# A new order table for a gated linear attention and gMLP kernel on one core

## The chip, the cores and the metric

The kernel runs on one core of a Trainium2 chip. The metric is the device time of one execution in microseconds (us); the median over runs is compared. A core has a matmul engine (TensorE, "PE" in the profile, with its weight loads as "PEld"), a vector engine (VectorE, "DVE"), a scalar engine (ScalarE, "ACT"), GpSimd ("POOL") and SyncE ("SP"), which only issues DMAs here. Each engine works through its own queue in order and waits for the others by semaphores. Matmuls write to PSUM, eight banks that DVE and ACT read; everything else lies in SBUF.

## The reference

Gated linear attention (a recurrence over time with a decay per key channel), and then a gMLP block with a spatial gating unit, on float32 inputs:

```python
B, H, S, D = 4, 8, 768, 48                      # attention
state = zeros(B, H, D, D)
for t in range(S):
    state = alpha[:, :, t, :, None] * state + einsum('bhd,bhe->bhde', k[:, :, t], v[:, :, t])
    y[:, :, t] = einsum('bhd,bhde->bhe', q[:, :, t], state)
x = y.transpose(0, 2, 1, 3).reshape(B, S, H * D)    # 4 x 768 x 384
h = maximum(x @ w_in, 0)                            # w_in 384 x 1024
u, v = h[..., :512], h[..., 512:]
v_n = (v - mean(v)) / sqrt(var(v) + 1e-6)           # over the last axis
v_s = einsum('ts,bsd->btd', w_spatial, v_n) + b_spatial[None, :, None]   # 768 x 768
out = (u * v_s) @ w_out                             # 512 x 384
```

## The kernel before

**Tiling.** A sequence of 768 is cut into six chunks of 128 steps; the four batches give 24 chunks, numbered 0 to 23 (chunk i belongs to batch i // 6). Inside a chunk the recurrence is done as matmuls: sums of log(alpha) along time, their exponentials folded into q and k, a masked score matrix, and a state that is carried from chunk to chunk. Chunks 0 to 9 are handled as pairs 0 to 4 (pair j is chunks 2j and 2j+1, their steps interleaved by parity), chunks 10 to 23 as singles. The names of the operations:

- Loads on SP: `ac`, `kc`, `qc`, `vc` are alpha, k, q and v of a pair, 384 KB each (with an `s` at the end: of a single, 192 KB). Three buffers of each kind, by pair number. `w_in.1`, `w_in.0`, `w_sp.0` to `w_sp.2`, `w_out` are weights of 768 KB, through two raw buffers, so that each waits for the `cast` operations of the one two before. `b_sp` is a small load that POOL issues.
- `ln` (ACT) takes the logarithm of alpha, `cum` (PE) sums it along time into a bank (with `tot`, the total, for pairs 3 and 4, whose second parity `c1` adds on DVE), `einv` and `eexp` (ACT) make exp(-sum) and exp(sum), the second in place in the bank, `ebc` (ACT) makes the exponential of the total from the same bank. A pair has each of `cum`, `einv`, `eexp` twice, by parity; so pair 0 has `einv.0.0` and `einv.0.1`.
- `kt` (POOL or DVE) and `qt` (DVE, out of the bank) multiply k and q; `vb` casts v. `tr.q`, `tr.k` (for a single `trk`) transpose on PE, `ev` (single: `evs`) copies out of PSUM on DVE or ACT.
- `sc` (PE) makes scores, `m` (single: `ms`, DVE) masks them, four per pair and two per single; `upd` (PE) makes the update of the state, `z` (DVE) adds the old state, `S` (POOL or DVE) scales it, `sb` casts it. `ya` (PE) is the part of a pair inside its chunks, `y` (PE) the part from the old state (for a single all of it), `xe` (ACT or DVE) copies the result out as the block's x.
- `v` and `u` (PE) are the two halves of the first projection, `ve` and `ue` (ACT or DVE) their relu, `bn` (DVE), `rs` (ACT) and `vn` (DVE) the normalisation. `s` (PE) mixes along time, in two parts; `se` (DVE) adds the bias, `g` (POOL or DVE) multiplies with u, `o` (PE) is the last projection, `oe` the copy out of its bank, `st` the store on SP. `s.b.d.h.m` has batch, feature tile, half of the time axis, part; `o.b.t` has batch and time tile.
- Set-up: `zeros` (DVE), `ident`, `tri`, `causal`, `one` (POOL) make masks and padding; `wt` (PE) transposes the spatial weights, `we` (ACT or DVE) copies them out; `bb` and `be` spread the spatial bias. `causal` must be over before the first `m` of a pair, `bb` needs the load `b_sp`.

**Order.** The whole program is 955 operations. A list of them is built in the order of the algorithm, each with the engines that may do it, the operations that it depends on and the PSUM banks that it takes. The order in which they are issued is a table written by a search outside the kernel: a string of words such as `P108@0:512#0`, that is engine letter (P PE, D DVE, A ACT, G POOL, S SP), number in the list, after `@` the bank or banks that it takes, and after each `:` a filler matmul of so many float32 columns into the bank named behind `#`. Filler keeps PE busy early on and computes nothing. The function that walks the table takes each word, asserts that dependencies and banks are met, and emits the instructions; each engine's queue then has its operations in the order of the table. The scheduler of the framework is switched off by `ctx.enter_context(tc.manual_schedule())`; it still sets a semaphore wait wherever two engines touch the same data, and where two engines read one PSUM bank.

The table before starts with pair 1, then pair 0, then pair 2; its first two lines:

```python
D2 D0 G4 S103 A107 P108@0:512#0:472#0 A110 S105 A111 D116 G5 G8 S53 S104 D1 G6 G7 P109@1 A112 A113 D3 D119
P124@0,2:512#2:384#2 D115 A57 P59@3 A62 A64 A114 D118 D126 P121@4,5 P58@6 A60 A63 A61 D122 D125 S54 D123 D68
```

Of the kernel before, what the change touches and what calls it, by code (L numbers as in the profile page):

```python
# [38 lines left out]


PLAN = """
D2 D0 G4 S103 A107 P108@0:512#0:472#0 A110 S105 A111 D116 G5 G8 S53 S104 D1 G6 G7 P109@1 A112 A113 D3 D119
P124@0,2:512#2:384#2 D115 A57 P59@3 A62 A64 A114 D118 D126 P121@4,5 P58@6 A60 A63 A61 D122 D125 S54 D123 D68
P134@5,0:384#7 S55 S162 S56 D69 P137@1,4 G65 D66 P74@6,3:400#7 A75 D136 D135 P49@2 P71@0,7 A72 D76 D73 P84@7,0:296#6
D139 D50 S9 S164 A166 P167@3 G67 G70 P77@2,4 P168@5 S106 S163 A10 A173 A169 A170 S13 D86 P87@0,6 D85 D89 D88
P90@0,6:512#7:112#7 A91 A171 G11 D78 G79 D12 P94@0:416#7 D138 D80 D175 S165 A172 G117 P92 A93 D81 D120 G82 G174 D178
P127@4,3 P183@6,1 P97@5 A185 A184 D177 P140@1,2 G83 P141 P180@6,7 D128 D129 G130 P51@4 G14 D95 D131 D182 A181 D96 P143
G179 D16 A144 A15 P193@6,7 D194 A142 P156@2 P190@3,0 A98 A52 D191 D195 D192 A157 P148@1 P150@5 G176 G132 A149 A133
D158 P186@3 P145@2 A146 P196@0,1 P154@7 D187 D188 S17 S20 G18 D147 P197 P152@3 D153 P31@2,4 D33 D99 G189 G21 G22 P199
A151 A19 A198 D155 P201@0 A200 A32 A159 A202 A100 D161 P214@1 A215 P204@2 P37@4,3 A38 P34@0,7 P216@5 P212@1 A36 D160  # L50
A217 S23 S319 A205 P40@4,6 A41 D101 D35 D39 D102 P230@7 P226@2 P218@4 D203 A42 G25 G24 P46@6,5 P222@3 D206 A207 D209
D208 S268 A213 D47 P43@1,0 P223 D224 D48 P227 A323 P231 D232 P219 P324@3 S26 G225 G233 D45 A272 A44 D228 P274@5 P273@1
P325@0 D275 P238@7 P239 P242@2 D326 S269 A331 A28 D220 G229 D27 G29 G221 D240 G241 S270 S321 P243 P246@4 P247 A276
A327 A278 A277 A30 A279 A280 D284 D244 P210@7 D248 D282 G281 P234@2 P235 D236 A328 S320 S271 G249 P253@1 A211 A329
A330 D333 D285 P287@7,4 G245 G237 A289 D288 D335 D336 P250@2 P290@5,3 D292 S379 P256@7 P341@4,6 S322 D343 A291 A251
A257 A254 P300@3,2 S403 G332 A342 G286 P303@0,5 P338@6,7 D301 D302 D305 P259@1 G283 P293@3,4 D294 G295 G296 A339 A340
G334 G337 S380 S381 P354@7,2 P351@5,6 S404 S405 S382 S570 S489 S406 A260 A383 P262@1 A263 P384@3 D304 S490 S572 D352
D297 D356 D355 P265@0 A385 S513 S491 S492 S546 S571 P306@1,5 P308 A407 A387 A309 A386 P344@2,4 P408@7 P313@5 D307
P310@1 G298 G299 G388 D353 D345 A409 G346 G347 S516 S515 S514 S611 G411 D266 D389 A314 D315 A311 A410 D412 D312
P357@2,6 P358 P391@1,3 P360 A359 S547 S548 S635 A393 A392 S613 S549 S612 P367@2 P365@3 A361 P398@1,7 A316 P414@0,5  # L60
D348 P373@6 G390 D400 D399 D318 P394@4 P369@7 A415 A416 A574 A374 A370 P417@1,5 S573 P371@0 S637 S636 P362@6 A372 A493
A363 P575@7 G349 G350 D395 P401@0 A402 G396 G413 D418 D419 D397 P420@5 P494@6 P422@0 D375 D364 A421 A576 D368 D317
P425@5 P431@2 A376 A423 D378 D377 A426 A497 D424 A495 A366 A577 P437@1 D427 A428 A432 A500 D438 D429 D430 A517 P451@0
A578 A496 A550 P443@5 P447@3 P439@4 P433@2 A434 G498 G579 P444 P448 P440 D580 D445 P435@7 P463@5 P464 P452 P518@2 A436
D441 D446 D449 A519 A520 D499 G442 P501@3,7 P582@6,4 D453 G454 D450 A583 A502 A521 A615 A524 P459@0 P504@1 D503 D505
D465 D523 P460 P467@6 P468 P551@5 D469 P508@1,3 G522 D461 P525@2,7 A552 A527 A526 D584 D509 D510 S614 S721 S638 A554
P471@6 P455@0 P456 P528@1 D457 A553 A472 P474@2 G466 G506 G462 A475 G555 P616@0 A639 A617 P532@6,3 D556 D529 P558@5,4
P589@2,7 S722 S745 D533 G458 G470 G507 G557 G620 P477@1 D590 D534 D591 S748 S724 S747 S723 S746 S778 P486@6 A560 A618
A478 A559 A619 A487 D621 P483@2 P561@1 A484 D530 G531 P511@7 D562 P535@5 P565@6,0 P623@3,4 D566 D567 D625 D624 A512
P640@2 G563 P537@7 A536 A641 P480@6 A538 A642 G581 S802 S781 S779 A564 P540@0 P585@3 G643 S780 D644 D586 S843 S804  # L70
S803 P568@4 P592@2 P630@3,7 P646@5,1 A541 A569 D542 P599@4 A593 S844 A648 A647 G622 P605@2 D539 P626@1 A606 A725 A481
A543 G587 G588 D631 P649@5,0 P594@3 P597@2 D627 D651 D632 G628 G629 G645 S845 S867 S805 P601@6 S868 S869 P726@7 P633@0
D650 A600 A595 P652@3 A727 A634 A749 D607 A653 P603@5 D596 D545 D544 A608 P654@0 A655 P657@3 D610 D609 A598 A658 D656
P665@4 A666 A728 A604 P750@0 P671@2 D659 A660 D661 D662 P667@3 D731 D732 A751 A753 A668 G756 A752 G730 G754 D755
P683@4 P663@5 A664 A602 A782 P679@1 P672 P669@3 D670 P684 D685 P680 P736@6 P675@3 P699@4 A729 D737 G738 D686 D681 G682
P783@6 P757@7,0 P733@1,5 P676 A784 A758 A786 A785 A734 A806 A759 A735 D673 D739 D674 D677 P760@2 P700 P695@7 P696 G789
G787 P691@3 P692 D761 G678 D701 D788 D697 G702 D693 P807@0 P790@6,4 D792 P740@5,7 P764@1,2 D765 D742 A808 A809 P687@3
P703@4 A847 A791 P793@6 P848@7 P688 P706@1 A704 A851 G698 P709@4 D812 A849 A810 A707 A850 G694 G762 D766 D794 D689
G811 G852 G763 P814@3,0 G795 G690 G813 D741 P797@1,6 P767@5 A710 A816 P743@4 A768 G796 D853 D815 P855@7,2 P821@3,0
D798 A744 A871 P772@5 D823 D799 D822 P769@4 P872@0 P817@6 A773 A857 A770 D818 D856 D774 P712@5 P715@3 P800@7 A873 A874  # L80
G875 A801 P824@6 D876 P862@4,2 P878@0,1 A825 A880 P833@7 D771 D879 P837@6 P829@0 D864 D863 S485 S846 S488 S870 S476
A713 G819 A775 A834 A830 A838 G820 G854 P858@2 D859 G860 G861 S255 S261 S708 S267 S252 S479 S714 S711 P881@5,1 S705
P718@4 P826@6 D882 D883 A877 A827 P865@5 P884@1 P835@6 D839 D828 A866 P886@5 P831@2 A885 A840 P889@1 P895@0 D887 D776
A832 P899@2 A836 A890 D777 D841 D842 A716 P915@1 P911@3 P919@6 P907@5 D888 D891 A892 D719 D894 D896 D893 P897@4 P903@7
P904 P916 P908 D905 G906 D898 P920 D917 P923@7 D909 D921 D922 S720 S482 S264 S473 S258 G910 S717 G918 P901@4 P912 D913
A902 A900 P927@5 P928 P931@2 D914 P924 P934@3 P940@4 A941 S942 P932 A935 S936 P937@6 A938 S939 D925 G926 D929 D930
D933 P949@4 A950 P952@2 P943@3 D944 A953 S954 S951 S945 P946@2 A947 S948
"""


# [867 lines left out]
```

## Time and profile before

| | |
|---|---|
| median of 3 runs (lowest to highest) | 145.87 us (145.28 to 146.18) |
| the profiled execution: its time, its span | 145.72 us, 143.9 us |
| granted PE clock over the span | 0.997 |
| busy time PE, PEld, DVE | 134.8, 80.6, 124.2 us |
| busy time ACT, POOL | 104.4, 81.1 us |
| matmuls, of them filler | 2225, 20 |
| moved by DMA | 28.66 MB |

The span runs from the first to the last instruction that the profiler saw; the execution's own time is 1.8 us longer. A busy time is the union of an engine's instructions, and matmuls overlap in the pipeline, so what an operation costs PE is better read as the distance from its start to the next one's start. A line of a group or a wait names engine, tile and line of the program, and most copies share one helper's line; the tile tells which operation it is (`vs` is written by `se`, `ptm` by `m` and `ms`, `kqT` by `ev`, `bc` by `ebc`, `binv` by `einv`, `zs` by `z`, `state` by `S`, `bank` by PE).

### The profile page before, as it was taken

To read this page: it belongs to the slowest core of one execution; us is meant where nothing else is said; L and a number is where in the kernel's file an instruction comes from. 1 tells how busy PE (TensorE), PEld (TensorE's weight loads), DVE (VectorE), ACT (ScalarE), POOL (GpSimd) and SP (SyncE) were. 2 spreads that over 40 slices of the span, in tenths; PEclk is the share of its full clock that TensorE was granted. 3 is DMA by queue.
4 is the path that set the end of the run, shared out by engine and by line. 5 is a ranking of instruction groups with operands and counts; after the bars stand their busy time and mean duration, and the time that the engine had idled before them with its cause. 6 is when DMAs were issued, how large, how long until landed. Compare 5 with 4: busy or idle time off the path is not lost.

```text
span 143.9 us, 5488 instructions
## 1 busy us (share of the span) xinstructions
PE 134.8 (94%) x2225; PEld 80.6 (56%) x2225; DVE 124.2 (86%) x282; ACT 104.4 (73%) x263; POOL 81.1 (56%) x121
## 2 busy tenths in 40 slices
PE   5999998999997999999999999999999999999990
PEld 2455545455564566556657675666656665566550
DVE  3099899999777899999999999998999999898950
ACT  3566384978939896799969998999597989640251
POOL 6063259743469949942538978562399965102610
PEclk9999999999999999999999999999999999999998
DMA  4999999857999999897979999998999964009054
GB/s 112 268 261 266 331 198 321 245 203 268 295 297 239 246 181 180 163 181 133 211 129 206 191 163 201 172 205 140 204 190 196 308 225 148 28 0 328 0 179 152
DMA packets 84841, 28.66 MB, mean 199 GB/s; under 512 B 79568, under 2 KB 83280, under 8 KB 84816
## 3 DMA queue, kind: packets, MB, share of 16 engines
q1 hardware_dynamic: 84784, 28.32, 88.0%
q8 instruction: 17, 0.28, 0.9%
q14 instruction: 8, 0.07, 0.1%
q0 software_dynamic: 32, 0.00, 0.0%
HBM read 23.60 MB, written 4.72 MB: 197 GB/s over the span
## 4 chain that ended last, share of the span: by engine, by line
PE 51%; ACT 8%; DVE 7%; issue 2%; DVEq 0%
PE bank L720 36%; PE bank L690 3%; DVE vs L855 3%; PE bank L662 2%; PE bank L706 2%; PE bank L372 2%; ACT v_sb L182 1%; PE bank L629 1%; DVE gT L187 1%; ACT uT L182 1%; PE bank L678 1%; PE bank L484 1%; PE bank L550 1%; ACT xT L176 1%; PE bank L527 1%
## 5 line engine op out<-in xcount | busy, mean ns | idle before, releaser
L720 PE MATMUL bank<-w_spT,vn 128*128 128x384 bf16 x192 | 35.6, 327 | 1.2 <-DVE vs L855 1.2
L187 POOL TENSOR_TENSOR gT<-vs,uT 128x384 bf16<-128x384 f32 x24 | 22.4, 948 | 16.8 <-DVE vs L855 16.7
L720 PEld LDWEIGHTS <-vn 128*128 128x128 bf16 x192 | 17.8, 97 | 12.9 <-issue 1.8
L187 POOL TENSOR_TENSOR kt<-kc,binv 128x384 bf16<-128x384 f32 x18 | 18.2, 1014 | 10.4 <-ACT binv L639 9.7
L187 POOL TENSOR_TENSOR state<-zs,bc 128x384 f32<-128x384 f32 x17 | 14.6, 857 | 10.1 <-DVE zs L350 5.5
L176 ACT COPY kqT<-bank 128x512 bf16<-128x512 bf16 x30 | 16.8, 590 | 4.4 <-PE bank L484 4.0
L720 PE MATMUL bank<-xT,w_in 128*128 128x384 bf16 x96 | 20.0, 327 | 0.0
L720 PE MATMUL bank<-w_in,xT 128*128 128x512 bf16 x72 | 18.9, 381 | 0.6 <-ACT bank L641 0.5
L720 PE MATMUL bank<-w_out_sb,gT 128*128 128x384 bf16 (+1 forms) x100 | 18.5, 321 | 0.2 <-DVE ptm L695 0.2
L695 DVE TENSOR_TENSOR ptm<-bank,mask 128x512 bf16<-128x512 f32 x28 | 17.9, 682 | 0.3 <-PE bank L690 0.2
L855 DVE TENSOR_TENSOR vs<-bank,bsp_bc 128x384 f32<-128x384 f32 x31 | 16.3, 548 | 2.0 <-PE bank L720 2.0
L187 DVE TENSOR_TENSOR qt<-qc,bank 128x384 bf16<-128x384 f32 x24 | 12.9, 546 | 5.3 <-ACT bank L447 4.7
L782 DVE BATCH_NORM_STATS2 stats<-v_sb 128x6 f32<-128x512 bf16 x24 | 16.3, 679 | 0.0
L182 ACT ACTIVATE uT<-bank 128x384 bf16<-128x384 f32 x25 | 11.7, 488 | 4.5 <-PE bank L720 4.4
L182 ACT ACTIVATE v_sb<-bank 128x512 bf16<-128x512 f32 x22 | 13.0, 598 | 2.5 <-PE bank L720 2.4
L535 DVE TENSOR_TENSOR ptm<-bank,mask 128x512 bf16<-128x512 f32 x20 | 12.9, 682 | 0.5 <-PE bank L527 0.4
L720 PEld LDWEIGHTS <-gT 128*128 128x128 bf16 x100 | 8.8, 98 | 5.9 <-issue 0.5
L720 PEld LDWEIGHTS <-w_in 128*128 128x128 bf16 x96 | 8.5, 98 | 6.4
L176 ACT CAST xT<-bank 128x384 bf16<-128x384 f32 x23 | 10.5, 484 | 2.1 <-PE bank L372 2.0
L234 PE MATMUL bank<-junk 128*128 128x512 f32 (+6 forms) x20 | 10.2, 624 | 1.9 <-DVE junk L277 1.8
L178 POOL CAST vb<-vc 128x384 bf16<-128x384 f32 x19 | 9.7, 523 | 3.9 <-DMA vc<-in_v_dram 3.9
L799 DVE TENSOR_SCALAR vn<-v_sb,mvs,rstd 128x512 bf16<-128x512 bf16 x24 | 9.2, 423 | 1.6 <-ACT rstd L793 1.5
(115 smaller groups left out, 246.4 us busy)
## 6 DMA issues: line engine op xcount, KB each, us to landing
ac<-in_alpha_dram SPq DMA_DIRECT2D x14, 192.0 KB, 5.1
kc<-in_k_dram SPq DMA_DIRECT2D x14, 192.0 KB, 4.6
qc<-in_q_dram SPq DMA_DIRECT2D x14, 192.0 KB, 4.3
vc<-in_v_dram SPq DMA_DIRECT2D x14, 192.0 KB, 4.7
raw_w<-in_moe_w_spatial_dram SPq DMA_DIRECT2D x3, 768.0 KB, 4.4
out_dram<-raw_w SPq DMA_DIRECT2D x11, 192.0 KB, 2.2
ac<-in_alpha_dram SPq DMA_DIRECT2D x5, 384.0 KB, 5.6
qc<-in_q_dram SPq DMA_DIRECT2D x5, 384.0 KB, 8.1
```

Source lines behind the costliest of these rows:

```text
L176: nc.scalar.copy(out=out, in_=in_)
L178: ENG[eng].tensor_copy(out=out, in_=in_)
L182: nc.scalar.activation(out=out, in_=in_, func=AF.Relu)
L187: ENG[eng].tensor_tensor(out=out, in0=in0, in1=in1, op=ALU.mult)
L234: nc.tensor.matmul(out=banks[n][:, 0:cols].rearrange("p (a b) -> p a b", a=4), lhsT=junk, rhs=junk[:, None, 0:cols // 4].to_broadcast([128 ...
L535: nc.vector.tensor_tensor(out=ptm[n2][:, par, s], in0=banks[sl.bank].rearrange("p (hp t) -> p hp t", hp=HP), in1=mask[:, par][:, None, :]. ...
L690: nc.tensor.matmul(out=pt[s][:, hp, :], lhsT=kT[rows, hp, :], rhs=qT[rows, hp, :], start=True, stop=True)
L695: nc.vector.tensor_tensor(out=ptm[n2][:, ci, s], in0=banks[sl_p[s].bank].rearrange("p (hp t) -> p hp t", hp=HP), in1=mask[:, 2][:, None, : ...
L720: nc.tensor.matmul(out=ps, lhsT=lhsT, rhs=rhs, start=first and n == 0, stop=last and n == len(pairs) - 1)
L782: nc.vector.bn_stats(out=stats[tt % 2], in_=v_sb[n2][:, tt, :])
L799: nc.vector.tensor_scalar(out=vn[n2][:, x, :], in0=v_sb[n2][:, x, :], scalar1=mvs[n2][:, x, 0:1], scalar2=rstd[n2][:, x:x + 1], op0=ALU.su ...
L855: nc.vector.tensor_tensor(out=vs[d], in0=banks[sl.bank][:, 0:TH], in1=bsp_bc[:, th, :], op=ALU.add)
```

## The change

Only the table is new: the same 955 operations, with other engines, banks and places. The functions that build and emit the operations are the same. The table after was found by a search whose model lets engines that read one PSUM bank wait for each other, and which judged an order with two sets of durations. Its first lines, which hold most of what the prediction walks through:

```diff
-D2 D0 G4 S103 A107 P108@0:512#0:472#0 A110 S105 A111 D116 G5 G8 S53 S104 D1 G6 G7 P109@1 A112 A113 D3 D119
-P124@0,2:512#2:384#2 D115 A57 P59@3 A62 A64 A114 D118 D126 P121@4,5 P58@6 A60 A63 A61 D122 D125 S54 D123 D68
...
+D0 D3 D1 D2 G5 G8 S53 S55 S103 S54 G4 A57 P58@0:512#0:512#0:160#0 A60 P51@1 A52 P59@2 A62 A61 A107 A63 S56 D66 D69
+P74@0,1:512#3:512#3:296#3 P108@3 S104 D65 G70 G6 D68 P71@4,5 A64 A76 A75 P109@1 A112 A110 S162 S105 D67 D72 D73
...
```

In names, the first operations of the new order by engine:

```
SP   ac.0 qc.0 ac.1 kc.0 vc.0 kc.1 ac.2 qc.1 vc.1 w_in.1 kc.2 qc.2 w_in.0 vc.2 ac.3 w_sp.0 qc.3 kc.3 w_sp.1 vc.3 w_sp.2
PE   cum.0.0 bb.1 cum.0.1 tr.q.0 cum.1.0 tr.k.0 cum.1.1 sc.0.1 upd.0 sc.0.0 cum.2.1 tr.k.1 bb.0 ya.0 cum.2.0 tr.q.1 y.1
     upd.1 sc.1.0 sc.1.1 v.0.0 v.0.1 tr.k.2 ya.1 y.3 tr.q.2 y.2 v.0.3 sc.2.1 v.0.2 sc.2.0 u.0.3.0 u.0.2.0 upd.2 u.0.0.0 ya.2
DVE  zeros.0 zeros.3 zeros.1 zeros.2 qt.0.0 qt.0.1 kt.0.0 kt.0.1 vb.0.0 ev.k.0.0 ev.k.0.1 m.0.1.0 m.0.0.1 z.0 S.0 m.0.1.1 z.1 m.0.0.0
ACT  ln.0 einv.0.0 be.1 einv.0.1 eexp.0.0 ln.1 eexp.0.1 ebc.0 ev.q.0.1 ev.q.0.0 einv.1.1 einv.1.0 ln.2 eexp.1.0 ev.k.1.0 ev.k.1.1 eexp.1.1
POOL ident b_sp tri vb.0.1 causal kt.1.1 kt.1.0 sb.0 S.1 cast.w_in.1.0 S.2 kt.2.0
```

and of the old one, on SP and PE:

```
SP   ac.1 qc.1 ac.0 kc.1 kc.0 qc.0 ac.2 vc.0 w_in.1 qc.2 vc.1 kc.2 w_in.0 vc.2 w_sp.0 w_sp.1 w_sp.2 ac.4 ac.3 w_out kc.3
PE   cum.1.0 cum.1.1 tr.q.1 cum.0.1 tr.k.1 cum.0.0 sc.1.0 sc.1.1 tr.q.0 bb.0 tr.k.0 sc.0.0 cum.2.0 upd.0 cum.2.1 sc.0.1 ya.0
     v.0.0 y.1 upd.1 tr.q.2 v.0.1 ya.1 y.2 tr.k.2 bb.1 y.3 sc.2.1 v.0.3 sc.2.0 u.0.0.0 u.0.1.0 upd.2 v.0.2 ya.2
```

Further on, the operations of pair 3 (tr.q.3, tr.k.3, sc.3.1, sc.3.0, upd.3, ya.3) go between batch 0's u, wt and first s, where they were behind all of batch 0's s. At the end PE's order was s.3.3.1.0, s.3.1.1.1, o.3.0, o.3.2, s.3.3.1.1, o.3.1, o.3.5 in two halves, o.3.3, o.3.4; it is now s.3.2.1.1, s.3.3.1.0, s.3.3.1.1, o.3.2, o.3.1, o.3.0, o.3.5.0, o.3.4, o.3.5.1, o.3.3.

Operations by engine, where the count differs (before, after):

| operation | DVE | ACT | POOL |
|---|---|---|---|
| xe | 1, 6 | 23, 18 | |
| ev | 10, 12 | 10, 8 | |
| kt | 6, 3 | | 4, 7 |
| kts | 0, 1 | | 14, 13 |
| cast | 3, 0 | 5, 6 | 8, 10 |
| sb | 3, 1 | 2, 5 | 15, 14 |
| S | 3, 2 | | 17, 18 |
| g | 8, 9 | | 24, 23 |
| vb | 1, 2 | 0, 3 | 9, 5 |
| vbs | 1, 2 | 3, 2 | 10, 10 |
| ue | 7, 6 | 25, 26 | |
| we | 6, 7 | 6, 5 | |
| be | 1, 0 | 1, 2 | |

Filler falls from 4000 columns in ten matmuls to 3656 in ten, the last of it ahead of tr.k.2 (before: of v.0.0).

## The prediction

> **What bounds the kernel now.** I read the busy times first, then the stretches, the chain that ended last, the waits, and last the timeline of each engine, to lay every operation of the table beside its time.
>
> ```profile
> span 143.9 us, 5488 instructions
> PE 134.8 (94%) x2225; PEld 80.6 (56%) x2225; DVE 124.2 (86%) x282; ACT 104.4 (73%) x263; POOL 81.1 (56%) x121
> ...
> PE bank L720 36%; PE bank L690 3%; DVE vs L855 3%; PE bank L662 2%; PE bank L706 2%; PE bank L372 2%; ACT v_sb L182 1%; PE bank L629 1%; DVE gT L187 1%; ACT uT L182 1%; PE bank L678 1%; PE bank L484 1%; PE bank L550 1%; ACT xT L176 1%; PE bank L527 1%
> ```
>
> The chain is mostly PE. But a pipelined PE looks fuller than it is, so I took from the timeline the distance from the start of one PE operation to the next (medians): v 0.653 us, u 0.489, a finished s 0.650 + 0.325, o 0.656, ya 0.668, tr 0.340, trk 0.331, sc about 0.33, a single's y 0.451. Over the 268 operations they add up to 121.7 us; ahead of the last one, 121.0. It starts at 139.40, so PE is then 18.4 us "late": lateness is start time less PE work ahead. It is the number that a new order can change. It is 5.3 at the first cum, 13.4 at the first v, 15.4 from 36 to 45 us, 17.65 at 68 us, and 18.4 at the end. Four fifths are the ramp.
>
> ```profile
> 0.00:5.00 5.00, 3.21 (x4) 1.33 (x5) 1.41 (x16) 1.83 (x2) 2.35 (x12) 1.00 0.66 159
> 5.00:10.00 5.00, 4.82 (x51) 2.39 (x49) 2.75 (x10) 2.90 (x7) 1.59 (x5) 1.00 1.27 261
> 10.00:15.00 5.00, 4.66 (x85) 2.58 (x85) 4.93 (x13) 3.52 (x11) 2.05 (x5) 1.00 1.23 277
> ...
> 60.00:70.00 10.00, 10.00 (x178) 6.05 (x175) 9.54 (x24) 9.82 (x26) 3.97 (x7) 1.00 0.92 174
> ```
>
> Stretches: after the first busy figure (PE) come PEld, DVE, ACT, POOL. DVE is full from 10 us on. Its own start-to-start times (m 0.60 us, qt and z 0.465, bn 0.82, vn 0.32) add up to 120.7 us: as much as PE. So I also count the "lead": DVE work that must be over before a PE operation, less PE work ahead of it. DVE's idle time plus the largest lead is a floor under PE's lateness. Before, the largest lead is 8.1 us, at batch 0's first s (behind vn.0.1), and DVE had idled 7.0 us by 28 us, its start included: 15.1, against a lateness of 15.4 there.
>
> ```profile
> DVE vs L855 <- PE bank L720: 2.0, 4, 0.8
> DVE kt L187 <- ACT binv L444: 0.9, 1, 0.9
> DVE qt L187 <- ACT bc L646: 0.5, 2, 0.3
> PE bank L720 <- ACT bank L641: 0.5, 1, 0.5
> PE bank L720 <- DVE vs L855: 1.2, 2, 0.9
> ```
>
> These waits, with what the chain shows around them, are PE's stalls after the ramp: 1.10 us before s.0.0.1.0 (45.2; a chain se, c1.3, ebc, einv, kt.3.1, se on DVE and ACT), 0.61 at cums.11 (57.0), 0.33 at v.2.0 (86.4), 0.40 at s.2.2.1.1 (105.9): 2.4 us in all.
>
> **The change, part by part.** No instruction is added or taken away, but for the filler: 4000 columns become 3656. Engines: DVE gains five xe (0.465), two ev (0.33) and a few others and loses three kt, three casts, two sb; by rows DVE +0.4, ACT +0.2, POOL +1.8 us. None is worth anything by itself.
>
> Bank reads. Two engines read one bank only where ebc (ACT) and qt (DVE) share it. ebc stands first in 13 of 16 cases in both tables. The row prices this: qt waited for bc twice, 0.5 us. Between 0 and 0.5 us of DVE time can come of it; I take 0. The Trainium skill (PSUM — Partial Sum Buffer, "PSUM bank collisions raise a hardware error") says that two engines on one bank and quadrant must be kept apart, reads against reads too; by that rule, with which the 0.5 us agrees, no order escapes and 0.5 us stays the most; without it the part is worth 0.
>
> Ramp, walked with the rows. zeros.0 now goes first on DVE, so filler starts at about 1.05 instead of 1.79, but ac.0 lands at 4.42 as ac.1 did: the first cum stays at 5.35. The granted clock rose at 6.44, 4.65 us after the first matmul; it may rise by 5.7. (By the Trainium skill, TensorE: Matmul & The Clock Gate, "What's actually happening", some 3.4 us of work are enough; the three large matmuls after the first would then be about 0.4 us sooner. The walk goes by the row.) bb.1 now stands second on PE and needs b_sp. That load took from 2.98 to 7.67; POOL now issues it at 1.3, so I put it at 6.0. Bounds: 3.3 (2 us, as a store takes, hidden) and 7.7, when cum.0.1, queued behind bb.1, and all after it would be 1.6 us later. On ACT be.1 and ln.1 now stand ahead of eexp.0.1: cum.0.1 done 7.1, einv.0.1 to 7.6, eexp.0.0 to 8.05, ln.1 (0.84) to 8.8, eexp.0.1 to 9.2, where eexp.1.1 ended at 7.83. So qt.0.1 ends at 9.8 and the first tr at 10.05 (before 9.08). kt.0.0 and kt.0.1 to 10.75, tr.k.0 to 11.0, vb.0.0 and two ev to 11.95: sc.0.1 starts at 12.0 (11.62). Then pair 0 goes through before pair 1: causal ends on POOL at 12.6, and DVE does m.0.1.0 to 13.25, m.0.0.1 to 13.9, z.0, S.0 and m.0.1.1 to 15.45, z.1 and m.0.0.0 to 16.5; ya.0 starts at 16.55 (18.92). Pair 1 pays for it: ln.2 waits for ac.2 (13.47), so eexp.1.1, behind two ev on ACT, ends at 17.0; qt.1.0 ends at 18.45, upd.1 starts at 19.3, m.1.1.1 ends at 23.3. On SP, w_in.1 goes past vc.1: 18.37 + 1.48 = 19.85 us; with ACT's two casts v.0.0 starts at 21.6 (20.63), with 1.0 us more PE work done: equal. The stores still go behind the last loads. kt.2.1, qt.2.1, qt.2.0, z.3, three ev, two bn and four m follow on DVE without a gap, so ya.2 starts at 30.25 with 15.3 us done: lateness 14.95 (15.06). No gain so far, and DVE has idled 9.0 us instead of 7.0.
>
> From there the lead decides. Pair 3's tr and sc now stand among batch 0's u and wt, and the lead peaks at 7.5 (sc.3.1, behind ev.k.3.1) and 7.7 (wt.5, waiting for se.0.2.0 to free its bank). 9.0 + 7.7 = 16.7 is PE's lateness at 45 us, 1.3 worse than before. But what follows is lighter: pair 4's kt are on POOL, five xe have spread, and leads are 5.3 to 5.7 through batch 1's v and u where they were 5.9 to 6.3. The walk finds DVE waiting 0.5 for c1.4 and 0.6 or less in places, still ahead of PE; on ACT xe.8 and xe.11 arrive 0.1 before they are needed. So 16.75 at 51 us of work, against 17.65: **0.9 us gained**. Its bounds are the walk's error, some thirty cross-engine steps: 0.7 lost to 2.2 gained.
>
> Turns. A large operation followed by a small one costs 0.095 more (v 0.742 against 0.648, o 0.745 against 0.650): the next weights are late. Such turns fall from 43 to 37: 0.57 us. Where DVE sets the pace nothing comes of it, so 0.4; bounds 0 and 0.6.
>
> Later stalls, 0.73 us after 68 us: leads in batches 2 and 3 are 0.2 to 1 us lower, so some go and others come; 0.2 gained, bounds 0.8 lost and 0.7 gained.
>
> Tail. The last s is now over 1.95 us of o before o.3.5.0, but g.3.3.1 and g.3.1.1 both follow it on DVE (0.55 to 0.7 each) behind se.3.0.1, ue.3.3.1 and se.3.1.1, and POOL does g.0.1 and g.2.1 late (0.914 to 1.226 each): o.3.5.0 waits 0.3; bounds 0 and 0.8. A full o, oe and a store end it as before.
>
> Sum: 0.9 + 0.4 + 0.2 - 0.3 = 1.2 us. The profiled execution took 145.72 us (1.8 around its span): 144.5. It lies 0.15 under the median of 145.87; I take 144.5 for the median too.
>
> **The rivals.** (a) The gain is larger: batch 1 to 3 run without stalls and the wait at wt.5 is shorter, as the later leads allow: 0.9 + 1.0 more, 143.5 and down to 143.0. For it: after 51 us of work DVE has 0.4 to 1 us to spare. Against it: ACT arrives with 0.1 us to spare.
>
> (b) The change doesn't do what it says: as many bank reads cross as before, and three engines that are full together give back in new waits what the order saves. Lateness at the end 17.6 to 18.6: 145.6, within 1%. For it: 0.5 us is all that the profile shows of bank reads, and the walk finds no gain until 45 us.
>
> (c) Slower: DVE's idle time in the ramp. Each qt, tr, ev, sc, m link of pair 0 and 1 lies across PE, and DVE cannot regain it before wt.5. Every microsecond beyond my 9.0 goes straight to PE: at 10.2 the change is worth nothing, at 12.0 it costs 1.8, so 147.5. A late b_sp alone gives 1.6 of that. For it: DVE already idles 2 us more than before, and POOL's causal now lies just ahead of the first m. Against it: loads land in the order of use, and the largest gap that I find is under 1 us.
>
> **How the numbers follow.** Forecast and (a) together are the gains, (b) is none, (c) a loss. The forecast has 0.35, (a) 0.19, (b) 0.24, (c) 0.22. A measurement of this kernel tells about 1%, or 1.46 us, from nothing; the forecast of 1.2 lies just short of it, so I give 0.23 of its 0.35 to faster and 0.12 to the same: faster 0.42, within 1% 0.36 with (b), slower 0.22. The range of the likeliest is 143.7 to 145.4; to hold 8 in 10 it must reach into (a) and (c): 143.1 to 147.5.
>
> **What would show it.** Right: first cum at 5.35, ya.0 near 16.5, v.0.0 near 21.6, ya.2 near 30.3, lateness near 16.7 from 45 us on, and few PE waits after that. Wrong: bb.1 or cum.0.1 after 6.5; ya.2 after 31.5 or DVE idle over 10.2 by then; new waits of PE on DVE vs, on ACT xT or on w_spT copies that add up to over 1 us; the last o waiting over 0.8 us on gT.

## The result, and the profile after

The kernel after takes 149.88 us (median of 4 executions, 149.66 to 152.21), beside 145.71 us for the kernel before on the same chip (4 executions, 145.28 to 146.18): a ratio of 1.030, with a 95% interval of 1.024 to 1.036. The new order is 3% slower. The prediction, 144.5 us in a range of 143.1 to 147.5, was wrong, in its sign too.

The first profiled execution ran 6.83 us of its start at half the granted clock, so the profile shown here is that of a second execution of the same kernel: 150.24 us, span 148.2 us, granted clock 1.000.

The page of the kernel after, busy times and the chain that ended last (shares of the span by engine, then by line):

```profile
span 148.2 us, 5462 instructions
PE 133.3 (90%) x2212; PEld 80.8 (54%) x2225; DVE 128.0 (86%) x283; ACT 104.3 (70%) x263; POOL 80.1 (54%) x120
...
PE 38%; DVE 28%; ACT 10%; SPq 6%; issue 6%; DMA 5%; POOL 3%; DVEq 0%; POOLq 0%
PE bank L720 26%; SPq L397 6%; DMA vc<-in_v_dram 5%; DVE vs L855 5%; DVE vn L799 4%; DVE gT L187 4%; DVE ptm L535 3%; DVE qt L187 3%; DVE stats L782 3%; PE bank L662 2%; PE bank L706 2%; ACT kqT L176 2%; DVE kqT L178 2%; PE bank L690 2%; ACT xT L176 2%
```

The chain of the kernel before, by engine:

```profile
PE 51%; ACT 8%; DVE 7%; issue 2%; DVEq 0%
```

Three things have moved. DVE is 3.8 us busier (124.2 before), with one instruction more. The chain, 51% PE and 7% DVE before, is now 38% PE and 28% DVE. (The chain before could be followed back only to 41.8 us, so its shares add up to 68%; of what was followed, DVE had about a tenth, and now has 29%.) And two DVE groups hold 8% of it that held 1% before: `vn`, which was not listed there, and `gT` (the operation `g`). The chain in order of time (start, length in us, engine, tile, line) has them in long pieces:

```profile
34.11 1.91 DVE vn L799 x2
...
77.35 1.20 DVE gT L187
...
104.62 2.08 DVE vn L799 x2
...
137.12 1.07 DVE gT L187 x2
```

The groups of instructions (count, busy us, mean ns of one, idle before) say the same over the whole program. First the kernel before, then the kernel after:

```profile
L799 DVE TENSOR_SCALAR vn<-v_sb,mvs,rstd 128x512 bf16<-128x512 bf16 x24 | 9.2, 423 | 1.6 <-ACT rstd L793 1.5
L187 DVE TENSOR_TENSOR gT<-vs,uT 128x384 bf16<-128x384 f32 x7 | 5.0, 713 | 0.2
```

```profile
L799 DVE TENSOR_SCALAR vn<-v_sb,mvs,rstd 128x512 bf16<-128x512 bf16 x24 | 11.9, 535 | 0.9 <-ACT rstd L793 0.8
L187 DVE TENSOR_TENSOR gT<-vs,uT 128x384 bf16<-128x384 f32 x8 | 8.3, 1051 | 0.0
```

The same 24 `vn`, with the same shapes, cost 2.7 us more; eight `g` cost 3.3 more than seven did, where one more at its undisturbed 0.55 us would be 0.55. The means hide two populations: most `vn` take 0.38 to 0.41 us, and six take 0.66 to 1.15. A view of one stretch shows what the long ones share. The timeline of the kernel after from 33.3 us, DVE and then POOL (start, length of the run of equal instructions, line, operation):

```profile
33.44 2.58 DVE L799 TENSOR_SCALAR vn<-v_sb,mvs,rstd 128x512 bf16<-128x512 bf16 x3
35.94 0.34 DVE L178 COPY w_spT<-bank 128x384 bf16<-128x384 bf16 x1
```

```profile
33.22 0.83 POOL L178 CAST w_row<-raw_w 128x768 bf16<-128x768 f32 x1
34.01 1.86 POOL L187 TENSOR_TENSOR kt<-kc,binv 128x384 bf16<-128x384 f32 x2
```

Three `vn` take 2.58 us where 1.2 would do. Instruction by instruction, `kt.3.0` on POOL ends at 34.96 and `vn.0.1` at 35.11; `kt.3.1` ends at 35.87 and `vn.0.0` at 36.02. The second place looks the same, DVE's `vn.2.4` and `vn.2.5` beside POOL's `kts.20` and `kts.19`:

```profile
104.62 2.06 DVE L799 TENSOR_SCALAR vn<-v_sb,mvs,rstd 128x512 bf16<-128x512 bf16 x2
```

```profile
104.70 1.83 POOL L187 TENSOR_TENSOR kt<-kc,binv 128x384 bf16<-128x384 f32 x2
```

So it is with all the long ones: the six long `vn` end 0.144 to 0.151 us behind a POOL instruction, and all eight `g` end 0.413 to 0.417 us behind one. The constant distance says that DVE does not slow down; it stands until POOL is done, and then needs its remaining time. Two more `vn` met only the last 0.20 and 0.17 us of a POOL instruction (`vn.1.0`, `vn.2.1`) and kept their 0.405 and 0.380 us. Counted so, 14 of DVE's `vn` and `g` are held in the kernel after for 7.1 us in all, and 5 in the kernel before (`vn.1.4` and four `g`) for 1.6 us. Other DVE operations that read SBUF alone are held too, and of these the kernel before has more: some 1.5 us (`sb.18` 0.57, `vbs.18` 0.26 and smaller ones), against 0.5 after (`kts.15`).

DVE's operations that read a PSUM bank beside one SBUF tensor keep their lengths in both kernels, POOL working or not (`m` and `ms` 0.68 us, `se` and `z` 0.55, `qt` 0.54), and so does `bn` (0.68 + 0.18).

### The profile page after: what moved, and what is told of

Its sections match the earlier page's. It is cut to its first block, busy times and chain, and to the rows that moved or that the text cites. A ratio compares the mean times of both kernels' runs of the same rounds, so it can differ in the third digit from the quotient of the medians.

```text
span 150.3 us, 5462 instructions
## 1 busy us (share of the span) xinstructions
PE 135.6 (90%) x2212; PEld 82.1 (55%) x2225; DVE 128.3 (85%) x283; ACT 104.3 (69%) x263; POOL 80.1 (53%) x120
## 4 chain that ended last, share of the span: by engine, by line
PE 42%; DVE 24%; ACT 10%; SPq 6%; issue 6%; DMA 5%; POOL 3%; DVEq 0%; POOLq 0%
PE bank L720 27%; SPq L397 6%; DMA vc<-in_v_dram 5%; DVE vs L855 5%; DVE vn L799 4%; DVE gT L187 4%; DVE ptm L535 3%; DVE stats L782 2%; DVE qt L187 2%; PE bank L662 2%; PE bank L550 2%; PE bank L706 2%; ACT kqT L176 2%; PE bank L690 2%; ACT xT L176 2%
## 5 line engine op out<-in xcount | busy, mean ns | idle before, releaser
L720 PE MATMUL bank<-w_spT,vn 128*128 128x384 bf16 x192 | 34.4, 326 | 1.7 <-DVE vn L799 0.9
L187 POOL TENSOR_TENSOR gT<-vs,uT 128x384 bf16<-128x384 f32 x23 | 21.7, 958 | 14.5 <-DVE vs L855 14.3
L176 ACT COPY kqT<-bank 128x512 bf16<-128x512 bf16 x28 | 15.5, 589 | 7.7 <-PE bank L662 6.4
L720 PE MATMUL bank<-xT,w_in 128*128 128x384 bf16 x96 | 19.2, 326 | 1.3 <-DVE w_spT L178 0.8
L187 POOL TENSOR_TENSOR kt<-kc,binv 128x384 bf16<-128x384 f32 x20 | 18.4, 934 | 2.2 <-ACT binv L639 2.1
L720 PE MATMUL bank<-w_in,xT 128*128 128x512 bf16 x59 | 18.1, 401 | 1.1 <-issue 0.4
L799 DVE TENSOR_SCALAR vn<-v_sb,mvs,rstd 128x512 bf16<-128x512 bf16 x24 | 11.9, 536 | 0.9 <-ACT rstd L793 0.8
L178 POOL CAST vb<-vc 128x384 bf16<-128x384 f32 x15 | 8.3, 561 | 7.2 <-DMA vc<-in_v_dram 7.2
L176 ACT COPY raw_w<-bank 128x384 f32<-128x384 f32 (+1 forms) x11 | 4.9, 470 | 9.4 <-PE bank L720 9.4
```

Of the source, the lines that this page charges most:

```text
L176: nc.scalar.copy(out=out, in_=in_)
L178: ENG[eng].tensor_copy(out=out, in_=in_)
L187: ENG[eng].tensor_tensor(out=out, in0=in0, in1=in1, op=ALU.mult)
L720: nc.tensor.matmul(out=ps, lhsT=lhsT, rhs=rhs, start=first and n == 0, stop=last and n == len(pairs) - 1)
L799: nc.vector.tensor_scalar(out=vn[n2][:, x, :], in0=v_sb[n2][:, x, :], scalar1=mvs[n2][:, x, 0:1], scalar2=rstd[n2][:, x:x + 1], op0=ALU.su ...
```

## The experiments

Two theories were to be told apart. **P, the theory of the shared work:** the order is as good as the prediction had it, but it makes DVE's `vn` and `g` coincide with POOL's instructions, and each holds the other up. **O, the rival:** the order itself is worse by 3 us or more (waits across engines, PSUM banks, loads), and long `vn` are a side effect that DVE's slack would cover.

**1. The kernel after, once more**, for a profile at full clock.

> The kernel after, unchanged, for a second profile. In its first profile vn took 0.54 us in the mean (before 0.42), up to 1.15, and g on DVE up to 1.27 (before 0.97), each time with a POOL operation running. Theory P (POOL holds DVE up): the long vn and g are at the same operations as in the first profile, 6 to 8 us in all over their undisturbed length, against 1.6 us before. Theory O (the order itself is slower): their lengths change from one execution to the next and the PE waits do not follow them. Both expect about 149.8 us.

It took 150.24 us. The operations that were long in the first profile are long again, at the same places and to within 8 ns: `vn.0.1` 995, `vn.0.0` 992, `vn.2.5` 997 ns. So their lengths belong to the order, not to chance.

**2 and 3. POOL's multiplications cut to an eighth, in both kernels.** The same edit in each, beside start values for what is then not written.

```diff
     def mul(eng, out, in0, in1):
+        if eng == "POOL":
+            few = tuple([slice(None)] * (len(out.shape) - 1) + [slice(0, out.shape[-1] // 8)])
+            out, in0, in1 = out[few], in0[few], in1[few]
         ENG[eng].tensor_tensor(out=out, in0=in0, in1=in1, op=ALU.mult)
```

> The kernel before with every multiplication on POOL (kt, kts, S, g) done on one eighth of its columns; the rest of those tiles keeps a start value. POOL then works for some 10 us instead of 56 on them. Theory P: DVE loses its 1.6 us of long vn and g, of which some reaches PE: 144.6 to 145.5 us. Theory O: the same, since the order is the old one.

> The kernel after with the same cut of POOL's multiplications. Theory P: vn falls back to 0.41 us and DVE's g to 0.55, some 7 us of DVE time go, and 4 to 5 us of the time: 144.3 to 145.8 us, level with or under the cut kernel before. Theory O: the waits lie in the order of the operations and in the ramp, so it stays 3 us or more over the cut kernel before: 148 us or more.

The kernel before with the cut took 144.20 us, a ratio of 0.990 (0.987 to 0.993), 0.4 less than P's range. The kernel after with the cut took 144.31 us, 0.989 (0.983 to 0.996), of the uncut kernel before. The order after becomes 5.6 us shorter by the cut, the order before 1.6, and the two are then level: O, which had the waits in the order itself, falls. The profile of the kernel after with the cut, its page and two groups:

```profile
PE 131.6 (93%) x2212; PEld 80.6 (57%) x2225; DVE 123.6 (87%) x285; ACT 103.9 (73%) x263; POOL 45.5 (32%) x125
```

```profile
L811 DVE TENSOR_SCALAR vn<-v_sb,mvs,rstd 128x512 bf16<-128x512 bf16 x24 | 8.8, 406 | 1.2 <-ACT rstd L805 1.0
L190 DVE TENSOR_TENSOR gT<-vs,uT 128x384 bf16<-128x384 f32 x8 | 4.5, 571 | 0.0
```

`vn` are back at 406 ns and `g` at 571, though not a line of DVE's work was changed. But the cut also makes POOL's own operations shorter (a `g` 0.35 us instead of 0.96), so POOL's results come earlier too. So an order that leaves POOL too little time is not excluded yet; the next runs go on from there.

**4 and 5. More POOL work in the kernel before.** Twelve extra 128x384 multiplications on POOL. In the first run each reads what `rs` writes, so it starts with the first `vn` of a couple; in the control it reads what the second `vn` writes, so it starts behind the couple.

```diff
+            nc.gpsimd.tensor_tensor(
+                out=load_out, in0=junk[:, None, :].to_broadcast([128, 3, 128]), in1=rstd[n2][:, tt:tt + 1, None].to_broadcast([128, 3, 128]), op=ALU.mult)
...
+                if x % 2:
+                    nc.gpsimd.tensor_tensor(out=load_out, in0=junk[:, None, :].to_broadcast([128, 3, 128]), in1=vn[n2][:, x, 0:384].rearrange("p (a b) -> p a b", a=3), op=ALU.mult)
```

> The kernel before with 12 extra POOL multiplications of 128x384, one behind each rs, so that each starts when the vn that wait for the same rs start; their results are not used. Theory P: most of the 24 vn grow from 0.42 to 0.7 to 1.0 us, DVE is busy 6 to 10 us longer, and the time grows by 3 to 6 us to 149 to 152. Theory O, in which POOL has time to spare (81 of 144 us) and its work costs nothing: under 1 us more, 145.5 to 146.7.

> The kernel before with the same twelve extra 128x384 multiplications on POOL as in the run that placed them at vn, but each reads what the second vn of a couple has written, so it starts when both are over. It is the control for that run (1.0698): the same 11 us of POOL work, and a wait in POOL's queue that ends even later. Theory of the shared work: vn keep 0.41 us (excess under 1 us where it was 4.1), some g and z nearby may be hit instead, and the time is 148 to 152. If the first run's loss came from POOL's queue alone, standing behind rs, the time is 156 or more here too, with vn short.

The first took 156.05 us (1.070, 1.063 to 1.077), 4 us more than either theory had it; the control took 151.42 us (1.037, 1.035 to 1.040), within its range, but with more than double the excess that was expected of its `vn`. Seven `vn` are long in the first (4.1 us of excess in all, `vn` mean 573 ns), four in the control (2.2 us, 494 ns), because an instruction that starts behind one couple still meets the next one. So the load did meet `vn`, and more of it cost more. But neither run is clean, as this line of the first one's groups shows (idle before, and its releaser, at the end):

```profile
L795 POOL TENSOR_TENSOR load_out<-junk,rstd 128x384 bf16<-128x384 f32 x12 | 10.6, 880 | 25.8 <-ACT rstd L794 24.2 <-PE bank L663 1.5
```

POOL stood 24.2 us in front of these instructions waiting for `rs`, and what lay behind them in its queue (`kts`, `S`, `vbs`) came late: PE waited up to 3.2 us at once for a bank that a masking operation (`ptm`) had to free. Of the 10 us, the part that is the meeting and the part that is the queue cannot be told apart. The control waited in the same way (17.4 us for `vn`), met half as much and lost 5.5 us, so the queue alone does not explain the first run's loss; that is as far as the two runs go.

**6. The same POOL work, only not at the same moment.** Two copies of one column are added to the kernel after. They make POOL's `kt.3.0` wait for `vn.0.0` and `kts.20` for `vn.2.5`, so until DVE is past four `vn`; nothing is moved or left out, POOL is only later.

```diff
+    def late_mul(eng, out, in0, in1, behind):
+        if eng == "POOL" and behind is not None:
+            nc.gpsimd.tensor_copy(out=after_vn, in_=vn[0][:, behind, 0:1])
+        mul(eng, out, in0, in1)
...
+                   0 if (j, par) == (3, 0) else None),
...
-        op(("kts", i), "POOL DVE", lambda e: mul(e, kt[:, :, :, 0:D], t["kc"], buf),
+        op(("kts", i), "POOL DVE", lambda e: late_mul(e, kt[:, :, :, 0:D], t["kc"], buf, 5 if i == 20 else None),
```

> The kernel after, with two one-column copies on POOL added: ahead of kt.3.0 it reads a column of what vn.0.0 writes, and ahead of kts.20 a column of what vn.2.5 writes. So POOL does the same work as before, but kt.3.0, kt.3.1, kts.20 and kts.19 start only when these vn are over. Theory of the shared work (POOL's operations hold up DVE's vn): vn.0.1, vn.0.0, vn.2.4 and vn.2.5, 0.99 to 1.15 us in the kernel after, go back to 0.41, a loss of 2.5 us on DVE disappears, wt.1 to wt.2 and s.2.2.0.1 start about 1 us sooner each, and though POOL is some 0.9 and 0.75 us later at these places the time falls to about 148 (147.2 to 148.8; ratio to the kernel before about 1.016). Rival (the order has too little slack for POOL, and its work comes late): two waits more on POOL make pair 3's keys and those of chunks 19 and 20 later, and the time rises to 151 to 152, with new PE waits at tr.k.3 and trk.19.

147.54 us (4 executions, 147.47 to 147.92), a ratio of 1.012 (1.010 to 1.014): **2.3 us faster than the kernel after (2.7 by the two ratios), by two waits more**, inside P's range and against O's 151 to 152. The four `vn` take 0.40 to 0.41 us. The stretch of the timeline shown above, now with the wait, DVE and POOL:

```profile
33.28 1.39 DVE L806 TENSOR_SCALAR vn<-v_sb,mvs,rstd 128x512 bf16<-128x512 bf16 x3
34.60 0.34 DVE L178 COPY w_spT<-bank 128x384 bf16<-128x384 bf16 x1
```

```profile
34.74 0.19 POOL L188 COPY after_vn<-vn 128x1 bf16<-128x1 bf16 x1 [0.85 <-DVE vn L806]
34.88 1.79 POOL L192 TENSOR_TENSOR kt<-kc,binv 128x384 bf16<-128x384 f32 x2
```

DVE's copy `w_spT` (`we.0.0`) starts at 34.60 instead of 35.94. POOL's two `kt` end 0.8 us later, at 36.67, and nobody waits for them: `tr.k.3` starts at 37.41, straight behind `wt.1`. PE's lateness at 20 us of work falls from 17.40 to 16.05. This run leaves POOL's speed and work as they were, but for two copies of 0.19 us, and makes POOL later, not earlier; it is the one that shows P. One more `g` came free with it, by the shift in time: `g.2.2.0` takes 0.55 us instead of 0.97.

**7 and 8. Five `g` on another engine**, alone and together with the two waits. `g.1.0.0` and `g.2.2.0` go from DVE to POOL, `g.3.0.0`, `g.3.3.0` and `g.3.2.1` from POOL to DVE.

```diff
-... A527 D442 P463@5 A576 P464 G450 D457 ...
+... A527 P463@5 A576 P464 G442 G450 D457 ...
-... G686 D682 D693 ...
+... G686 G682 D693 ...
-... P924 G906 G918 D909 D914 D910 ...
+... P924 D906 D918 D909 D914 D910 ...
-... G922 D926 D935 G930 A941 ...
+... G922 D926 D935 D930 A941 ...
```

> The kernel after, with five g on another engine: g.1.0.0 and g.2.2.0 go from DVE to POOL, g.3.0.0, g.3.3.0 and g.3.2.1 from POOL to DVE, so that in these places one engine alone multiplies. DVE has one g more than in the kernel after. Theory of the shared work: the g of DVE that is left in the tail take 0.55 to 0.6 us instead of 1.03 to 1.27, four of them in a row end sooner than the two that had POOL beside them did (138.9 instead of 139.3 us), se.1.0.1 is no longer 0.65 us late for s.1.1.1.0, and the time falls by 1.0 to 1.8 us, to about 148.5 (ratio about 1.020). Rival (what counts is how the work is divided): DVE, which sets the pace, gets 0.47 us more, POOL's help in the tail is missed, and the time rises by 0.5 to 1.5 us, to 150.4 to 151.4.

> Both edits together: the two waits on POOL and the five g on another engine. Theory of the shared work: their gains add, DVE's excess over undisturbed lengths falls from 7 us to about 2, and the time comes to about 146.5 (145.6 to 147.3; ratio about 1.005): most of what the new order lost is back without any work left out. It does not reach the 144.3 of the kernel after with POOL's multiplications cut to an eighth, since g.0.0.1, g.0.3.1, vn.0.2, vn.1.1 and g.1.3.1 still meet POOL. Rival: 150 or more.

149.84 us (1.032, 1.027 to 1.037) alone, and 147.83 us (1.013, 1.011 to 1.015) with the waits: no gain over the kernel after, and none over run 6. Both forecasts missed by 1.3 us, and the rival's 150.4 or more did not come either. The local part came as P has it. Where the tail of the kernel after had `g` on both engines, DVE's two and POOL's two,

```profile
137.03 2.28 DVE L187 TENSOR_TENSOR gT<-vs,uT 128x384 bf16<-128x384 f32 x2
```

```profile
136.80 2.10 POOL L187 TENSOR_TENSOR gT<-vs,uT 128x384 bf16<-128x384 f32 x2 [10.66 <-DVE vs L855]
```

DVE alone does all four in two runs of 1.03 and 1.02 us (run 8):

```profile
134.03 1.03 DVE L192 TENSOR_TENSOR gT<-vs,uT 128x384 bf16<-128x384 f32 x2
...
135.44 1.02 DVE L192 TENSOR_TENSOR gT<-vs,uT 128x384 bf16<-128x384 f32 x2
```

That is 2.05 us of one engine's time for four (with a `se` between the pairs, 2.4 us from start to end), against 2.5 us (136.80 to 139.31) for four on two. And the 0.82 us wait of PE at `s.1.1.1.0` is gone. What ate the gain were queues. On POOL, `g.2.2.0` pushed `kts.21` back, and PE waited 1.06 us for it at `trk.21` (0.58 in run 6). On DVE, `g.3.2.1` had been put behind `oe.18`, which waits for `o.3.2`; PE then waited 1.00 us for this `g` inside `o.3.5.0`, where it had waited 0.39 us for another `g` in the kernel after. (The expectations put this wait at `o.3.4`, the next operation to start.)

**9 and 10. The moves mended.** With the two waits: only `g.1.0.0` goes to POOL, and `kts.21` goes ahead of `g.2.3.0`; in the second run the tail's three `g` go to DVE as well, `g.3.2.1` now ahead of `oe.18`.

```diff
-... D685 G686 D682 D693 A808 A809 G811 D812
+... D685 D682 D693 A808 A809 G811 G686 D812
-... G922 D926 D935 G930 A941 ...
+... G922 D926 D930 D935 A941 ...
```

> The kernel with the two waits on POOL (147.54), and two edits of the table: g.1.0.0 goes from DVE to POOL, ahead of g.1.2.0, and POOL does kts.21 ahead of g.2.3.0. The tail is left as it is in the kernel after. Theory of the shared work: s.1.1.1.0 no longer waits 0.82 us for se.1.0.1, and trk.21 waits 0.1 instead of 0.58 us for kts.21, so 146.4 (146.0 to 146.9; ratio 1.003). Rival (what POOL is given in one place is lost in the next, as trk.21 did with the five moved g): 147.2 or more.

> The same, and in the tail g.3.0.0, g.3.3.0 and g.3.2.1 on DVE, the last of them now ahead of oe.18, which held it for 0.7 us in the run with the five moved g. Theory of the shared work: PE's waits in the tail, 0.64, 0.27 and 0.39 us at o.3.2, o.3.1 and o.3.4 with POOL's help, become 0.39, 0.27 and 0.3 at most, so 146.0 (145.5 to 146.5; ratio 1.000). Rival (DVE needs POOL's help there): the waits come to 1.6 us again as with the five moved g, and 146.7 or more.

147.18 us (1.008, 1.005 to 1.011) and 146.81 us (1.007, 1.004 to 1.010): 0.4 and 0.7 us under run 6, each about 0.8 short of what was expected: the first stands at the edge of its rival's range, the second inside it. The 0.4 is not clear of noise (the interval of run 6 is 1.010 to 1.014). `s.1.1.1.0` and `trk.21` wait no more. But PE now waits for POOL's `g.2.2.1`, inside `o.2.3`, so that `y.19` behind it starts at 114.6 us with 0.65 us more lateness, a loss that run 6 did not have. The group of `o` in run 10 (idle before, and its releaser, at the end):

```profile
L727 PE MATMUL bank<-w_out_sb,gT 128*128 128x384 bf16 (+1 forms) x100 | 18.4, 320 | 1.0 <-POOL gT L192 0.4
```

So the 0.58 won at `trk.21` is gone again, as the rival there had it. In the tail of run 10 the waits at `o.3.2` and in `o.3.5.0` shrink, from 0.64 to 0.17 and from 0.39 to 0.29 us. But `s.3.3.1.0` now waits 0.39 us for its bank, which `se.3.1.0` frees, and this `se` stands on DVE behind two of the `g` that were moved there. No version that does the whole work beat the kernel before.

## Why the prediction was wrong, point by point

PE's lateness (its start time less its work ahead), the quantity of the prediction, read from the traces at the same amount of PE work:

| us of PE work done | before | forecast | after | run 6 (two waits) | run 3 (POOL cut) |
|---|---|---|---|---|---|
| 15 | 15.06 | 14.95 | 14.79 | 14.64 | 14.63 |
| 20 | 15.26 | | 17.40 | 16.05 | 15.73 |
| 30 | 15.41 | 16.7 | 18.55 | 17.20 | 16.88 |
| 50 | 17.66 | 16.75 | 18.98 | 17.36 | 16.60 |
| 70 | 17.75 | | 20.22 | 18.59 | 16.47 |
| 90 | 18.24 | | 21.61 | 18.32 | 16.20 |
| 115 | 18.30 | | 21.60 | 18.82 | 16.20 |
| 120.9 (the end) | 18.38 | 17.2 | 22.98 | 20.20 | 16.15 |

(The forecast's 17.2 is 18.4 less its sum of 1.2.)

**The ramp was right.** The first cum started at 5.51 us (5.35 forecast), `sc.0.1` at 11.73 (12.0), `ya.0` at 16.72 (16.55), `v.0.0` at 21.87 (21.6), `ya.2` at 30.55 (30.25); `b_sp` landed at 5.76 (6.0) and `w_in.1` at 19.82 (19.85). Lateness at `ya.2` was 15.20, forecast 14.95. DVE had idled 9.3 us by then, where the forecast had 9.0 and rival (c) needed more than 10.2. So rival (c), which put the loss into that idle time, is refuted although its sign was right.

**The step that failed is the use of DVE's times.** "Its own start-to-start times (m 0.60 us, qt and z 0.465, bn 0.82, vn 0.32) add up to 120.7 us" were taken from the old order and carried over to the new one as if they belonged to the instructions. For `m`, `qt`, `z` and `bn` they do. For `vn` and `g` they belong to the instruction and to what POOL does at that moment: `vn` took 0.38 to 1.15 us, `g` 0.54 to 1.27. The profile before had the sign in it: `vn.1.4` took 0.80 us, and four of the seven `g` 0.68 to 0.97. The walk then said "9.0 + 7.7 = 16.7 is PE's lateness at 45 us" (30 us of work in the table). It was 18.55, and most of the difference is one place: between 15 and 20 us of work the two `kt` of pair 3, which POOL now does among batch 0's u and wt, meet `vn.0.1` and `vn.0.0`, and lateness grows by 2.6 us. With the two held apart (run 6) it grows by 1.4 there and is 17.20 at 30 us of work; with POOL cut (run 3) that is 16.88. The walk to 50 us of work, 16.75, is near what run 3 shows: 16.60. Three of PE's longest waits in the kernel after show the path (total, times, longest); `w_spT` is `we.0.0` behind the long `vn`, for whose bank `u.0.3.1` waits:

```profile
PE bank L720 <- DVE vs L855: 1.2, 2, 0.7
PE bank L720 <- DVE vn L799: 1.1, 3, 0.6
PE bank L720 <- DVE w_spT L178: 0.8, 1, 0.8
```

**"By rows DVE +0.4, ACT +0.2, POOL +1.8 us. None is worth anything by itself"** is the same error in the counting of engines. DVE's busy time rose by 3.8 us, not 0.4. DVE has three `kt` less (four went to POOL, `kt.0.0` came; 0.55 us each, 1.65 in all), and one of the four, `kt.3.1`, cost DVE 0.59 us at `vn.0.0` instead.

**A rule that the prediction passed over.** Every held instruction of the kernel after ends 0.15 or 0.41 us behind POOL's, and operations with one input in PSUM are not held. The Trainium skill states this (SBUF — State Buffer, "SBUF: two separate sides" and "Who interferes with whom"): DVE and GpSimd share one pair of SBUF ports as an exclusive lock, DVE takes it when it works in a two-port mode or reads two SBUF tensors, and whichever comes second stands still until the first is over; DVE with at most one SBUF input outside these modes does not contend. The trace agrees, with a refinement: `vn.2.4` started 0.09 us ahead of `kts.20` by the profile and was held all the same, and `vn.1.0` started 0.63 us behind POOL's `S.10` and was not lengthened, so the visible start does not always decide. The prediction cited the bank rule, which was worth 0.5 us at most, and not this one, by which it would have had to count where DVE and POOL meet.

**Turns: not settled.** Forecast 0.4 us. The counts, 43 and 37, hold, and an `o` before a small operation takes 0.743 us in both kernels; but a `v` there takes 0.657 in the kernel after, no more than before a large one, so its price was not a constant. In run 3 lateness falls from 16.60 at 50 us of work to 16.15 at the end, which holds the turns and the later stalls together.

**Later stalls: wrong**, 0.2 us gained by the forecast, at worst 0.8 lost. From 50 to 115 us of work lateness grew by 2.6 us: 0.82 at `s.1.1.1.0` (`g.1.0.0`, 1.27 us), 1.28 at `s.2.2.0.1` and `s.2.1.0.1` (`vn.2.4` and `vn.2.5`, 2.1 us together), the rest in steps under 0.4. Run 6 takes away the second, runs 7 to 10 the first.

**Tail: the forecast wait came, two others were missed.** The forecast had `o.3.5.0` wait 0.3 (0 to 0.8) for two `g` "(0.55 to 0.7 each)". PE waited 0.39 us there, for `g.3.1.1`, which took 1.03 us: right in place and size. But two `g` earlier took 1.09 and 1.27 us on DVE, and behind them `se.3.2.1` came late to free the bank of `o.3.2`, which waited 0.64 us. `o.3.1` waited 0.27 us for the bank that `ue.3.3.1` frees; it does so in run 10 too, where neither of the two `g` is held, so this wait belongs to the order. That makes 1.30 in all.

**What stays open.** Of the 5.6 us that the cut of POOL's multiplications is worth to the kernel after, run 6 shows 2.3 to be the meeting of DVE and POOL. The 0.7 that run 10 gains beyond it come from fewer meetings and from changed queues together. The other 2.5 us hold six more held instructions (`vn.0.2`, `vn.1.1`, `g.0.0.1`, `g.0.3.1`, `g.1.3.1`, `kts.15`: 2.2 us of excess in the kernel after), and also POOL's results, which the cut brings forward; no run parts them. Nor does any run show why the full order, mended as in run 10, is still 1.1 us behind the kernel before.

## What to carry to other kernels

An operation's duration can belong to what another engine does at that moment, not to the operation: before costing a move between VectorE and GpSimd, lay both timelines side by side and count what will coincide with what. In the groups of a profile, a mean that differs between two orders of the same instructions is the sign to look for, and the end times tell the cause: a constant distance behind the other engine's end says that the instruction waited, and was not slow. A wait that keeps two such engines apart can be cheaper than the overlap (2.3 us here), but each move shifts a queue, so what stands behind it has to be counted as well.

## What the runs showed of the hardware that was not expected

Both sides lose. POOL's `g` and `kts` (128x384) take 0.91 us alone, and 1.22 to 1.23 us in the kernel after where a DVE `g` was on (`kts.10`, `g.1.3.0`, `g.3.3.0`); in run 6 a `g` of DVE that started in the same 10 ns as POOL's kept its 0.549 us, and POOL's took 1.315. These are the three `g` that follow each other there on POOL, 0.92 + 1.32 + 0.91 us:

```profile
105.67 3.06 POOL L192 TENSOR_TENSOR gT<-vs,uT 128x384 bf16<-128x384 f32 x3
```

The new order can lose PE's clock in the ramp. In the first profiled execution PE's granted clock fell to half at 18.64 us for 6.83 us, behind a stretch with little PE work (3.77 us busy of 5, where the kernel before has 4.71); in run 10's it fell near 21 us for about 3.4 us. The stretches of that first execution (the third figure from the right is the granted clock):

```profile
15.00:20.00 5.00, 3.77 (x124) 2.49 (x123) 3.31 (x7) 3.90 (x10) 1.40 (x3) 0.86 1.15 311
20.00:30.00 10.00, 9.38 (x208) 5.54 (x209) 8.03 (x17) 6.20 (x16) 5.63 (x9) 0.73 1.13 303
```

That execution took 152.21 us, 2.3 more than the median of its kernel. In a second execution with the same stretch as thin (3.78 us busy of 5) the clock stayed at 1.00. So the same work shows both. The Trainium skill (TensorE: Matmul & The Clock Gate, "What's actually happening") tells of a free-running activity window of some 3.4 us; the lengths of both falls, two and one such windows, agree with it.
